# Merged RWKV and gMLP kernel: one early decay scan instead of two, weight checks in halves from the middle on, and five more constant products at the start

## The chip, the cores and the metric

The kernel runs on one core of a Trainium2 chip. The metric is the device time of one execution in microseconds (us). TensorE (PE) multiplies matrices; VectorE (DVE), ScalarE (ACT) and GpSimd (POOL) work on elements; SyncE (SP) issues nearly all DMAs. PSUM is the memory that PE writes to.

## The reference

```python
for t in range(768):                                   # batch 4, 8 heads, head size 48
    cur = einsum('bhd,bhe->bhde', u * k[t], v[t])
    y[t] = einsum('bhd,bhde->bhe', r[t], state + cur)
    state = w[t][..., None] * state + einsum('bhd,bhe->bhde', k[t], v[t])
x = y as (4, 768, 384)
h = gelu(x @ w_in)                                     # 384 -> 1024, tanh form
u_, v_ = h[..., :512], h[..., 512:]
v_n = (v_ - mean) / sqrt(var + 1e-6) * g_ln
v_s = einsum('ts,bsd->btd', w_sg, v_n) + b_sg          # mixes the 768 tokens
out = x + (u_ * v_s) @ w_out                           # 512 -> 384
```

The decays w lie between 0.8 and 0.95. w_in and w_out come in as 64-bit floats, all else as 32-bit floats.

## The kernel before

**Recurrence.** The 768 tokens of each of the 4 sequences are cut into 6 chunks of 128, which gives 24 steps, numbered 0 to 23. A step loads the decays W with a guard column ahead of each of the 4 head pairs (4 blocks of 129 columns and a closing one, 517 in all), and K and R side by side in one buffer KR. `decays` makes the products of the decays: a scan from the right writes the suffix products Suf (line 568, restarted at the guards by constants), and a second scan turns W into prefix products that start from the reciprocal of a block's whole product. `decayed_k` multiplies K by Suf (617), and the last part of `decays` multiplies R by the new W (585). PE then transposes K (`turned`, 724), multiplies K by R (`scores`, 678), forms K times V (`products`, 685) and adds up the outputs (701, 712). `own_weights` makes the term with u: for steps 0 to 3 by a product on DVE or POOL (629) and 8 small matmuls (634), later on the element engines; `masked` lays the scores over it (755).

**The second scan.** For steps 0 to 7 it runs in two halves of 258 columns. Each half has a reciprocal of 2 guards ahead of it, written into a PSUM tile called `resets`, whose other columns are zero, and the scan computes state = W * state + resets. For steps 8 to 23 it runs in one piece, with 4 reciprocals written into an SBUF tile D2 of 517 columns. Line 568 likewise takes its restart constants from `resets` (as bf16) in the early steps and from D1 in the later ones. After step 7 `resets` becomes a fourth PSUM tile for large products.

**gMLP.** Outputs of three steps make half a sequence. `taken` copies it out of PSUM, `move` shifts rows with small DMAs (918), `split_x` cuts it into a high and a low part. `v_piece`, `u_piece`, `gate_piece` and `out_piece` form every large product as three matmuls of high and low parts (950, 951, 952). For the last sequence sums of tokens replace part of the products. Weights are cut in two by `f64_weight` (DVE lines 1303 to 1311, three matmuls at 1315 to 1317 for the first six) or `f32_weight`.

**Checks.** The fast path holds for weights and decays within a range. `range_check` reads the decays of two steps again and squares and compares them on ACT (603, 605); `f64_check` reads each of the 10 pieces of the 64-bit weights again into a KR buffer and does the same (1339, 1340). Both begin after the last step's K. `verdict` adds up the counts on DVE (1263 to 1275), sums over partitions by a 1-column matmul (1278), writes `bad` (1280), and every engine loads that flag and branches (1431, 1433).

**Order.** Each function is a chain of operations, and `ORDER` lists which chain takes its next operation on which engine (S, P, D, A, G for SP, PE, DVE, ACT, POOL); every engine runs its instructions in that order. A planner in the kernel keeps an assumed time for each operation; from it come the buffer each one takes, waits of POOL on earlier DVE work, and constant matmuls with which `fill` (481) covers planned gaps of PE in the first 80 us. Ahead of all this `warm` issues `WARM[0]` constant products of 128 columns on an all-ones tile. In `own_weights` two more precede the 8 small matmuls.

Of the kernel before, what the change touches and what calls it, by code (L numbers as in the profile page):

```python
# [8 lines left out]
F32 = mybir.dt.float32  # L9
# [6 lines left out]
ALU = mybir.AluOpType  # L16
# [9 lines left out]
DM = H * D  # L26
# [17 lines left out]
f3D f3D k4S q1S k4D v1P v1A x1P D1D f3D D1D f3D e3G k4D k4D k3S k3D q2S o4S t0S t0S t0S k2P k2A H2P a3A H2A d2A j4A  # L44
v1P z2P w3P F1A F1A C0A k4D k4P k3D f3G h2S h2A h2G s2D w3D r4S x2P f4D k5S c0S D2D D2D f4D w3A f4D f4D v2P v2A p4S
C0P d3A z3P v2P e4G C0A s3D k5D k3D F2A F2A k4A k5D h0S t1S t1S t1S p5S k3D w4D k5D r5S C1A C1D w4D w5D H3P H3A h0A
j3A h0G j5A a4A K0P K0P K0P K0A H4P v3P v3A x3P w5G D3D w4D H4A w4A h1S q4S o5S h1A k3P f5D f4D D3D t2S h5S t2S t2S
K1P K1P v3P x4P f5D k5D K0D d4D f4D e5G D4D D4D f5D a5A k3A C2A C2D h1D F3A h5A F3A k5P h5D k5A h3S h3A h3G K0A K0G
K1P K1A o6S h4S h4A q5S z4P q6S p6S J1P H5P J1P H5A J1P f5D s4D v4P v4A f5D w5D w5A r6S t3S k6S o8S t3S t3S J2P J2P
J2P x5P v4P K1D K1A h4D d5D f5D D5D z5P f6D s5D f6D K0G w6G J0P J0P J0P K1G F4A F4A v5P J2A K0G K0A K1G K2P e6D J0A  # L50
k6D w6D k6D K1D k6D v5A v5P K0A C3A C3D j6A k6D K0D k6D k8S k8D o7S r7S F5A F5A t4S t4S t4S p8S k6D k8D J1A K1A K1A
K1D k8D f7D H6P H6A t5S t5S t5S C4A C4G K2P K2P j8A K2A K2D k8D e7D k8D K3P K3P K3P K3A K3D K2A K2D k8D C5A C5G J3P
J3P J3P J3A K3A a7G K3G K2G K4P x6P H7P H7A q8S D6A f6D w6D w6A K3G K2G K3G K3A K2A f6D f6D f6G K4P K4P D6D f7D f7D
f7D f7D k9S k9D f7D k9D k9D k7S q7S k9D K2A K2D w8D J4P J7P J7P J4P J4P J4A k7D k7D J7P J7A K3A K4A K4D K4A K3D j7A
k7D k7D K4D k7D p7S r9S r8S z6P s6D K4G J6P J6P J6P m1P j9A w7D K5P K5P K5P K5A K5D K5A m1P m1P m1P m0P K4D K4A k9D
k7D k9D m0P m0P m0P z7P J6A K5D w8D w7D w8D w7D K5G K5G K4A K4D f8D K5A K5A K5D m2P m3P m3P m2P m2P f8D f8D f8G w7G
m0P m3P m3P m0P m0D m0D m0A e8G m1P m1P m1D a8A m0D m1D m1A s7D p10S o9S p9S r10S f9D w8A m2P m2P m2P m2D m3P m3P J5P
d7A J5P J5P J5A m1D m2D m2A m3D m3D m3A a9A m2D f9D E6P w9G e9G w10G m3D f9D f9G u0P u1P u0P u1P u2P u1P u2P u1P u0P
u0P o10S r11S q9S F6A I8A D7D F6A s8D D7D E7P w9D w9D w9A d8A F7A I9A F7A w10D w10D f10D e10G u1D f10D f10D f10G s9D
D8D D8D w10A a10G u0D m7P m7P m7P m4P p11S o11S f11D f11D f11D f11D m7P m7P m7P m7D E8P F8A m4P F8D w11D w11D p12S u1S  # L60
r12S q10S u2P u2P w11D u2D e11G d9G m4P w12G w12G m4P m4P m4P m5P m5P m5P m5P m6P m5P m6P I10A q11S t6S t6S t6S m7D
m4D D9D m4D D9D s10D o12S w11A f12D m7A C6A a11G d10G m7D C6D f12D f12D E9P F9A I11A e12G F9A m4A C7A C7G f12G m6P m6P
m6P K6P K6P m6P m5P r13S p13S u0S o13S s11D D10D w12D q12S u2S r14S D10D m4D m6D f13D m6D f13D K6P K7P K6A m6A m6D
w12A a13G C8G C8G w13D K6G w13D f13D f13D K7P E10P J11P K7P d11G K6A K7A K7G K7A J11P J11P J8P J8P K8P K8P K8P J11A
F10D F10D D11D s12D m5D m5D K6G K6G K6G e13G f14D K7D q15S p14S o14S I12A E11P J8P r15S o15S K6A K6A K6D m5A m5D K7G
K7G K8A w13D w13D f14D F11A F11A a14A J8A I13A K8G K8A t7S t7S q13S t7S J9P u5P J9P J10P J10P J10P J10A J9P w14D f14D
K7D K7A f14D w14D s13D w14D K8G K8G K8D f15D f15D J9A K7D C9A C9D e14D C10G C10G e15G u4P K8A K8A u3P u3P u3P p16S
p15S u4P u4P u4P u4D u5P u5P u5P u3P r16S u5D u5S C11A D12A D12D K8D C11D w15D w15D K9P K9P K9P K9A K9D d13A E12P f15D
K9A K9G K9G I14A K9G w14A D13D f15D D13D q14S a15G K9A K9A u3D F12D w16D f16D s14D J15P J15P K11P K11P K11P J15P K11A
K11G F12A K11A K9D m9P K10P K10P K11D K11G w16D K10P K10A J15A r17S K10G m10P E13P K11D K11G K11G w15D w16D d14A K10A  # L70
K10G K10G F13D F13A K10D f16D m10P m10P K11G m9P m9P m10P m8P w15D K10A K10A K10D a16G o17S o16S p18S u4S p17S q16S
u3S f16D m8P m8P m8P m8P m8P m8D m8D I15A D14D D14D f17D m8A m8D s15D e16G f16G m9P m11P m11P m9P m9P m9D m9D m9A m9D
e17G f17D m11P m10P m10P m11P m11P m10D m10D m10A m10D J12P m11P m11D d15A E14P J14P J14P m11D F14D F14A u6P u6P u6P
J14P J14A w18G w16G w18G w18D f17D f17G s16D m11A m11D J12P J12P J12A u8P D15D D15D w17D I16A a17A w17D d16D r18S p20S
# [290 lines left out]
def rwkv_gmlp(ctx: ExitStack, tc: tile.TileContext, wpad, kr, vtok, ktok, vt, u, ucol, w_in, consts_, w_sgT, w_out, out):  # L365
# [196 lines left out]
    def decays(n):  # L562
# [7 lines left out]
        if early:  # L570
# [6 lines left out]
            if n == RESETS - 1:  # L577
                m_m.free.append((op.seen, resets))
# [1032 lines left out]
```

## Time and profile before

| | us |
|---|---|
| median of 3 runs (range) | 347.82 (347.13 to 348.28) |
| profiled execution: its time | 350.2 |
| profiled execution: first to last instruction (span) | 348.4 |
| PE busy | 340.0 (98%) |
| DVE / ACT / POOL busy | 273.0 / 213.5 / 148.2 |

The profiled execution took 1.8 us more than its span, and 2.4 us more than the median of the runs without a profile. A busy PE means that some matmul was under way; other engines may be idle at no cost while PE is the bound.

### The profile page before, as it was taken

How to read it: one execution, taken by the hardware profiler on the slowest of the kernel's cores; microseconds unless marked ns; L12 is line 12 of the kernel's file. 1: busy time of each engine (PE TensorE's matmuls, PEld its weight loads, DVE VectorE, ACT ScalarE, POOL GpSimd, SP SyncE). 2: the span in 40 equal slices, each digit the busy share in tenths (PEclk: the TensorE clock that was granted, in tenths of full speed). 3: DMA queues.
4: the chain of work that ended last, by engine and by line, in shares of the span. 5: the costliest groups of instructions: out<-in, count | busy, mean ns of one | idle time of the engine just before them, and what ended most of it. 6: DMA issues, size and time to landing. Idle time of an engine off the chain costs nothing.

```text
span 348.4 us, 10988 instructions
## 1 busy us (share of the span) xinstructions
PE 340.0 (98%) x4453; PEld 313.9 (90%) x4453; DVE 273.0 (78%) x541; ACT 213.5 (61%) x564; POOL 148.2 (43%) x221
## 2 busy tenths in 40 slices
PE   7999999999999999999999999999999999999994
PEld 6887688899999899889999989999999889999993
DVE  6989999998999799777889796866746365767673
ACT  1579799972664477572313375372642689897982
POOL 7356343505524541453707445144323634448400
PEclk9699999999999999999999999999999999999998
DMA  7868995614256737235256345220365454636742
GB/s 287 300 225 288 345 337 186 189 56 158 85 170 215 236 130 236 68 105 206 76 163 202 115 147 197 96 100 36 119 205 173 155 182 164 232 125 192 201 147 95
DMA packets 28470, 60.46 MB, mean 174 GB/s; under 512 B 3456, under 2 KB 13184, under 8 KB 28416
## 3 DMA queue, kind: packets, MB, share of 16 engines
q1 hardware_dynamic: 28272, 59.63, 51.5%
q8 instruction: 36, 0.59, 0.7%
q14 instruction: 18, 0.15, 0.2%
q10 hardware_dynamic: 144, 0.10, 0.1%
HBM read 53.82 MB, written 4.72 MB: 168 GB/s over the span
## 4 chain that ended last, share of the span: by engine, by line
PE 91%; ACT 3%; POOL 2%; DMA 2%; DVE 1%; issue 0%; SPq 0%; POOLq 0%; ACTq 0%
PE m_ps L950 17%; PE m_ps L952 16%; PE m_ps L951 16%; PE resets L950 6%; PE resets L951 6%; PE resets L952 6%; PE a_ps L678 5%; PE y_ps L701 4%; PE y_ps L712 3%; PE y_ps L685 2%; DMA x<-y 2%; PE m_ps L481 2%; PE m_ps L1145 1%; PE a_ps L1145 1%; PE m_ps L724 1%; PE y_ps L1145 1%
## 5 line engine op out<-in xcount | busy, mean ns | idle before, releaser
L950 PE MATMUL m_ps<-wsgh,vn 128*128 128x384 f32 x114 | 39.1, 343 | 0.0
L952 PE MATMUL m_ps<-wsgh,vn 128*128 128x384 f32 x114 | 38.4, 337 | 0.0
L951 PE MATMUL m_ps<-wsgl,vn 128*128 128x384 f32 x114 | 38.3, 336 | 0.0
L653 ACT ACTIVATE a<-KR,own 128x64 f32<-128x64 f32 x120 | 30.4, 342 | 4.1 <-DVE own L647 4.0
L617 POOL TENSOR_TENSOR KR<-KR,W 128x512 f32<-128x512 f32 x18 | 21.8, 1216 | 23.6 <-DVE W L568 8.1
L950 PE MATMUL m_ps<-g,wouth 128*128 128x384 f32 x80 | 27.3, 341 | 0.0
L952 PE MATMUL m_ps<-g,woutl 128*128 128x384 f32 x80 | 26.9, 336 | 0.0
L951 PE MATMUL m_ps<-g,wouth 128*128 128x384 f32 x80 | 26.9, 336 | 0.0
L1050 ACT CAST g<-m_ps 128x384 fp32r<-128x384 f32 x21 | 9.9, 477 | 27.0 <-DVE m_ps L1048 27.0
L950 PE MATMUL m_ps<-xT,winh 128*128 128x384 f32 x75 | 25.9, 345 | 0.0
L952 PE MATMUL m_ps<-xT,winl 128*128 128x384 f32 x75 | 25.2, 336 | 0.0
L951 PE MATMUL m_ps<-xT,winh 128*128 128x384 f32 x75 | 25.2, 336 | 0.0
L987 POOL TENSOR_TENSOR st<-st,mhalf 128x1 f32<-128x1 f32 x24 | 14.7, 613 | 20.2 <-DVE g L1322 6.3
L678 PE MATMUL a_ps<-KR 64*64 64x128 f32 (+1 forms) x768 | 22.8, 255 | 0.0
L1046 DVE SCALAR_TENSOR_TENSOR m_ps<-m_ps,flat 128x384 f32<-128x384 f32 x21 | 13.0, 618 | 12.1 <-PE m_ps L952 11.3
L950 PEld LDWEIGHTS m_ps<-wsgh,vn 128*128 128x128 f32 x114 | 21.4, 188 | 0.6
L583 DVE TENSOR_TENSOR_SCAN W<-W,D 128x516 f32<-128x516 f32 x16 | 21.4, 1337 | 0.4
L952 PEld LDWEIGHTS m_ps<-wsgh,vn 128*128 128x128 f32 x114 | 21.4, 188 | 0.3 <-DVE vn L1002 0.3
L701 PEld LDWEIGHTS y_ps<-a,vtok 64*64 64x64 f32 x768 | 16.0, 134 | 6.2 <-issue 3.9
L951 PEld LDWEIGHTS m_ps<-wsgl,vn 128*128 128x128 f32 x114 | 21.4, 188 | 0.2
L701 PE MATMUL y_ps<-a,vtok 64*64 64x64 f32 x768 | 21.2, 224 | 0.0
L585 POOL TENSOR_TENSOR KR<-KR,W 128x512 f32<-128x512 f32 x12 | 14.8, 1231 | 14.3 <-PE m_ps L952 3.7
(374 smaller groups left out, 1095.7 us busy)
## 6 DMA issues: line engine op xcount, KB each, us to landing
KR<-in_kr SPq DMA_DIRECT2D x24, 512.0 KB, 4.5
RK<-in_ktok SPq DMA_DIRECT2D x20, 384.0 KB, 4.2
W<-in_wpad SPq DMA_DIRECT2D x24, 258.5 KB, 3.1
KR<-in_wpad SPq DMA_DIRECT2D x9, 517.0 KB, 3.8
vtok<-in_vtok SPq DMA_DIRECT2D x24, 192.0 KB, 3.8
out<-o SPq DMA_DIRECT2D x21, 192.0 KB, 2.7
vn<-in_w_in SPq DMA_DIRECT2D x6, 512.0 KB, 4.8
KR<-in_w_in SPq DMA_DIRECT2D x6, 512.0 KB, 4.1
```

The costliest lines, as they stand in the source:

```text
L583: nc.vector.tensor_tensor_scan(W[:, 0:WL - 1], W[:, 0:WL - 1], D2[:, 0:WL - 1], 0.0, ALU.mult, ALU.add)
L585: engine[op.e].tensor_tensor(cols(x.R), cols(x.R), blocks(W, 0), ALU.mult)
L617: engine[op.e].tensor_tensor(cols(x.K), cols(x.K), blocks(x.Suf, 2), ALU.mult)
L653: nc.scalar.activation(a[:, j, p], eyes, AF.Copy, scale=o[:, j, p:p + 1])
L678: nc.tensor.matmul(ps_[64 * c_:64 * c_ + 64, j, p * C:p * C + (2 * T if c_ < turn else T)], x.K[rows, at:at + T], r_, start=True, stop=True)
L701: m = nc.tensor.matmul(place(y, j, q, r, c_), x.V[64 * c_:64 * c_ + 64, h * D - up(p, j):h * D - up(p, j) + 64], x.a.tile[64 * c_:64 * c_ ...
L950: nc.tensor.matmul(ps, lh, rh, start=(i == 0), stop=False)
L951: nc.tensor.matmul(ps, lh, rl, start=False, stop=False)
L952: nc.tensor.matmul(ps, ll, rh, start=False, stop=(i == n - 1))
L987: nc.gpsimd.tensor_tensor(rstd, var, c.mhalf, ALU.pow)
L1046: nc.vector.scalar_tensor_tensor(ps, ps, c.g[:, d:d + 1], c.b_bc[:, ts], ALU.mult, ALU.add)
L1145: nc.tensor.matmul(ps, x, y, start=False, stop=True, skip_group_check=True)
```

## The change

It has five parts.

1. In the early steps the second scan runs in one piece, as in the later ones. In both, the 4 reciprocals go into the guard columns of W itself, and the scan computes state = W * state + 0 from an initial 1: at the end of a block the state is its reciprocal start times the block's whole product, that is 1 up to rounding, so the next guard restarts it. The zeros come from one column of `resets` (early) or D1 (later), read with step 0. The reciprocal no longer waits for the scan of the step before, and the tile D2 with its memset leaves the recurrence.
2. `f64_check` runs on half pieces, 20 instead of 10, takes the free tile D2 instead of a KR buffer, and may start after step 8's K instead of the last step's.
3. `range_check` reads two steps in one DMA from step 2 on, not only from step 6 on (13 DMAs instead of 15).
4. `WARM` has 16 constant products instead of 11.
5. `ORDER` is another list. The engines of many operations differ in it: R times W goes to POOL 17 times instead of 12 and K times Suf 15 times instead of 18; `decayed` leaves DVE (5 times before) for POOL and ACT; the first product of step 1's `own_weights` goes from POOL to DVE; step 0's K goes from DVE to POOL and step 1's from POOL to DVE. In the first steps scores come ahead of transposes on PE, and `k0`, `o2`, `o3` are loaded earlier. At the end the verdict's 7 DVE operations ahead of its matmul come before the last pieces are finished, the 1-column matmul follows the last large one at once, and four of the last six output DMAs go to ACT's queue (one before).

```diff
-r0S o0S w0G f0D f0D f0D f0D f0D e0D r1S b0S f0G f1D k1S k1D k1D w0P w0A w0A a1A j1A o1S q0S k2S r2S H0P z0P w1G w1P
-w1A H0A w1A f1D f1D f1D k1D k1D k1P s0D f1D e1G k2D f1D k2D k0S k0D k2D k0D v0P H1P z1P s1D k0D x0P k2D k0D f2D f2D
-f2D o3S j2A j0A v0A D0A D0D H1A v0P F0A a2A F0A k1A o2S q3S k0P k0A d1A w2G w2P w2A w2A w3G e2G f2D f2D r3S f2G f3D
...
-u23P u22P u21P u22P u19S u18D u18S u23P u21P u21P u22P u23P u21P u21D u21S u22P u22D u22S u23P u23D u23S u23D u23A M0D
-M0D M0D M0D M0D M0D M0D M0P M0D
+r0S o0S r1S b0S w0G w0P w0A w0A f0D f0D f0D f0G e0G f1D f1D f1D k1S k1D o1S z0P w1D k0S q0S H0P H0A k1D s0D o2S o3S
+r2S f1G k1D e1D j1A a1A w1P w1A w1A v0P v0A z1P k1D k1P r3S k0D k0D k0D k0D j0A s1D k0P k1A f2D f2D f2D x0P k5S k0A
+a2A D0A D0D H1P H1A k2S d1A f3D q2S q1S w2G w2P w2A v0P w3G x1P e2G f2G k2D f3D k2D k5D D1D k5D k2D k5D k2D F0A F0A
+k5D e3G k4S w2A f3D v1P v1A w3P v1P H2P j5A f3G j2A F1A F1A H2A h1S h1A h1G r4S D1D k2P k2A d2A z2P o4S t0S t0S t0S
...
+J31A A1D A0A A0D u23P u21P u22P u22P A1D M0D u18D M0D A1A A1D u18S u19A M0D M0D u21P u23P u21P u23P u22P u22P u22D
+u22A u21P u21D u21A u23P u23D u23A u23D M0P u23S M0D
-WARM = (11, 80.0, 0.22)
+WARM = (16, 80.0, 0.22)
...
-    r_two = resets[:, 0:HQ]
+    r_zero = resets[:, 0:1].broadcast_to([128, WL - 1])
+    d_zero = D1[:, 1:2].broadcast_to([128, WL - 1])
-    nc.vector.memset(D2, 0.0)
...
-        if early:
-            for i in range(2):
-                at = slice(i * HQ, (i + 1) * HQ)
-                yield Op({"DVE": 0.1}, after=[ch[n - 1].e_pre] if n else [])
-                nc.vector.reciprocal(r_two[:, 0:HQ:Q], Suf[:, i * HQ + 1:(i + 1) * HQ:Q])
-                op = yield Op({"DVE": 0.64}, done=x.e_pre if i else None)
-                nc.vector.tensor_tensor_scan(W[:, at], W[:, at], r_two, 0.0, ALU.mult, ALU.add)
-            if n == RESETS - 1:
-                m_m.free.append((op.seen, resets))
-        else:
-            yield Op({"DVE": 0.12}, after=[ch[n - 1].e_pre] if n else [])
-            nc.vector.reciprocal(D2[:, 0:WL - 1:Q], Suf[:, 1:WL - 1:Q])
-            yield Op({"DVE": 1.17}, done=x.e_pre, two=True)
-            nc.vector.tensor_tensor_scan(W[:, 0:WL - 1], W[:, 0:WL - 1], D2[:, 0:WL - 1], 0.0, ALU.mult, ALU.add)
+        yield Op({"DVE": 0.12})
+        nc.vector.reciprocal(W[:, 0:WL - 1:Q], Suf[:, 1:WL - 1:Q])
+        op = yield Op({"DVE": 1.17}, after=[ch[i].e_pre for i in range(n)] if n == RESETS - 1 else [], done=x.e_pre,
+                      two=not early)
+        nc.vector.tensor_tensor_scan(W[:, 0:WL - 1], W[:, 0:WL - 1], r_zero if early else d_zero, 1.0, ALU.mult, ALU.add)
+        if n == RESETS - 1:
+            m_m.free.append((op.seen, resets))
...
-        two = n < 6
+        two = n < 2
...
-        op = yield dma(n, take=[s_kr], after=[ch[N - 1].e_k])
+        op = yield dma(n, take=[s_d2], after=[ch[RESETS].e_k])
-        yield Op({"ACT": 1.55}, free=[b], done=e_wchk[k])
+        yield Op({"ACT": 0.52 + n / 500}, free=[b], done=e_wchk[k])
...
     for k, w in enumerate(weights):
-        plan.add(f64_check(k, w[1]))
+        for i in range(2):
+            n = w[1].shape[1] // 2
+            plan.add(f64_check(2 * k + i, w[1][:, i * n:(i + 1) * n]))
```

## Rows read from the trace of the kernel before

**Rows 1.** The profile page: the chain that ended last, by engine.

```profile
PE 91%; ACT 3%; POOL 2%; DMA 2%; DVE 1%; issue 0%; SPq 0%; POOLq 0%; ACTq 0%
```

**Rows 2.** Busy time by stage: length, engines (instructions), granted clock, DMA share, GB/s.

```profile
0.00:45.00 45.00, 41.97 (x687) 34.06 (x687) 38.82 (x82) 29.29 (x97) 23.76 (x47) 0.92 0.85 292
45.00:100.00 55.00, 55.00 (x780) 49.57 (x779) 52.28 (x108) 41.88 (x119) 22.29 (x28) 1.00 0.51 168
100.00:280.00 180.00, 179.76 (x2640) 169.26 (x2639) 137.55 (x255) 88.36 (x246) 77.20 (x107) 1.00 0.45 147
280.00:343.00 63.00, 63.00 (x349) 60.98 (x347) 42.66 (x90) 54.01 (x104) 24.99 (x40) 1.00 0.54 175
```

The engines stand in the order PE, PEld (weight loads), DVE, ACT, POOL.

**Rows 3.** The same view, stretches of 2 us in the head.

```profile
6.00:8.00 2.00, 1.30 (x10) 1.11 (x10) 1.48 (x4) 0.00 (x0) 1.36 (x2) 1.00 1.00 394
8.00:10.00 2.00, 2.00 (x11) 1.79 (x10) 1.97 (x4) 1.15 (x6) 1.18 (x1) 0.52 0.80 319
...
14.00:16.00 2.00, 2.00 (x14) 1.86 (x13) 2.00 (x5) 0.23 (x2) 0.07 (x1) 0.78 1.02 390
```

**Rows 4.** The chain that ended last, head: start us, us, what.

```profile
6.11 1.26 POOL RK L629
...
11.15 3.71 PE m_ps L481 x16
...
18.76 1.31 PE m_ps L481 x10
...
31.47 6.17 DMA x<-y
```

**Rows 5.** Timeline of the head: start us, us, engine, line, what [idle before].

```profile
1.28 4.32 PE L481 MATMUL m_ps<-junk 128*128 128x128 f32 x22 [1.28 <-POOL junk L458]
...
3.84 1.23 DVE L568 TENSOR_TENSOR_SCAN W<-W,resets 128x516 f32<-128x516 f32 x1 [0.86 <-DMA W<-in_wpad]
...
5.10 0.17 DVE L574 RECIPROCAL resets<-W 128x2 f32<-128x2 f32 x1
...
6.24 0.69 DVE L576 TENSOR_TENSOR_SCAN W<-W,resets 128x258 f32<-128x258 f32 x1
...
9.14 0.49 DVE L1303 TENSOR_SCALAR vn<-vn 128x512 int32<-128x512 int32 x1
...
9.66 0.69 DVE L1305 SCALAR_TENSOR_TENSOR vn<-vn,vn 128x512 int32<-128x512 int32 x1
...
18.06 0.69 PE L678 MATMUL a_ps<-KR 64*64 64x64 f32 x32
...
18.89 0.74 DVE L755 COPY_PREDICATED a<-mask,a_ps 128x512 f32<-128x512 uint8 x1 [2.07 <-ACT winh L1328]
...
40.42 1.22 DVE L568 TENSOR_TENSOR_SCAN W<-W,resets 128x516 f32<-128x516 f32 x1
```

**Rows 6.** Single lines, the full-width scans: count, ns min/median/max, first and last start.

```profile
L568 DVE TENSOR_TENSOR_SCAN W<-W,resets x8: 1202/1222/1229, 3.8 to 60.6; 128x516 f32<-128x516 f32 x8
...
L583 DVE TENSOR_TENSOR_SCAN W<-W,D x16: 1220/1226/2058, 83.1 to 237.7; 128x516 f32<-128x516 f32 x16
```

**Rows 7.** ACT by line and shape, weight checks: busy us, mean ns, idle before.

```profile
L1340 ACT ACTIVATE KR<-KR,hmin 128x512 f32<-128x512 f32 x6 | 4.6, 769 | 0.2
L1339 ACT ACTIVATE KR<-KR 128x512 f32<-128x512 f32 x6 | 4.0, 670 | 3.2 <-DMA KR<-in_w_in 3.2
...
L1339 ACT ACTIVATE KR<-KR 128x384 f32<-128x384 f32 x4 | 2.2, 561 | 5.0 <-DMA KR<-in_w_out 5.0
```

**Rows 8.** The chain that ended last, its end.

```profile
343.73 0.09 DVE chk L1263
...
344.91 0.15 DVE bad L1280
```

**Rows 9.** The line of the branch, SP's part: count, ns, first and last start.

```profile
L1433 SPq EVENT_SEMAPHORE  x8: 17/17/17, 346.1 to 346.7; - x8
```

**Rows 10.** DMA issues from 342 us on: count, KB each, us to landing.

```profile
out<-u ACTq DMA_DIRECT2D x1, 96.0 KB, 1.9
```

More of the change, by code (lines that the diff above doesn't have):

```diff
@@ L46 @@
[L46 to L50, printed above, removed]
@@ new lines @@
+D3D f5D D3D f5D j3A a4A v3P a5A d4A x4P K0D k3D K0A w4D K1P K1P h4S h4A p5S k3D k3P e5G w5G D4D w4D w4A F3A F3A f5D
+f5G k4D D4D h3S h2S t2S t2S t2S k3D h5S o8S r6S q5S h4D C2A C2D w5D p6S q6S h3A h3D K1P K0G K0G K0G H5P z4P w5D s4D
+K1A H5A K1D h5A h5D k5P k5A h2A h2G d5A J2P J2P J0P J0P v4P x5P f6D D5D v4D f6D f6D K2P K2P z5P v4P w6G w6D o6S k6S
+t3S t3S r7S t3S w5A K0A s5D F4A F4A K0A J2P J2A K2P w6D f6G k8S v5P v5A e6D k6D K0D k6D K1A K1D C3G f7D J0P J0A J1P
+t4S t4S t4S K1G v5P k6D K2A C3D F5A F5A j6A k6D o7S r8S t5S J3P H6P H6A K2D K2A k8D k6D f7D K1G C4A K1A K1A k6D f7D
@@ new lines @@
+J1P J1P J3P K2G K2G K2G K2A C4D t5S t5S k8D k8D K1D k8D j8A C5A C5D k8D J3P x6P K3P K3P K3P K3A K3D k8D K2A J3A K2D
+K3A K3D f8D K3G D6A D6D f8D q8S k7S k7D k7D p7S q7S p8S K4P K4P K4P K4A J6P J6P J6P J6A J4P J4P w6A k7D K4D k7D K4A
+K3D e7D w8D K4D K4G J5P J4P J4A j7A z6P K5P K5P K3A K3A J1A a7A J5P J5P J5A H7P K5P s6D f7D k7D K4D K3D w7D k9S z7P
+m1P m1P m1P k9D k7D k9D r9S K5A a8A K5D j9A k9D k9D k9D k9D w7D K5A H7A K5D w8D w7D K5G K5G m0P m1P m0P m0P m0P K4A
+K4A f9D K4D f9D f8D K5A K5A K5D w7A m3P m3P w8D w8A s7D m2P m3P m2P m2P m2P f8G p10S o9S p9S m2P m0P m3P m3P m0P m0D
@@ new lines @@
+u10P u10P u10D e20G K12P u9P J18P u9P u9P K12P u9D J16P J16P e21D I19D K14D f21D p22S i19S t9S q20S D18A t9S t9S u10S
+r22S J16P J16A D18D K12P K12A K12D d19G C15G K12A a21A J17P J17P J17P J17A u11P u11P u11P u11P C15D K12G K12G C16A
+u11D C16G E18P w22D K13D C17A C17D K15P K15P f21D F18D F18D J18A i19A K12G K12G K12A K15P K15A I20D w21A s20D f22D
+f22D D19D D19D i8S r23S q21S o22S w23G w23D w23D K15D K15A K17P K17P J20P J20P J20P J20A K17P K16P K16P K16P K12D E19P
+J22P J22P J22P K15D K15G K15G K16A a22A K16D d20G K15A f22D K15A K15D f22D K16A K17A D20D D20D e22G d21A J22A K17G
@@ new lines @@
+K17A J23P J23P K16D K16G m17P m17P J23P J23A m18P s21D f23D F19D F19D I21A m16P m17P m16P E20P m19P m16P K17G K16G
+f23D K17G K17D K16G K16A w22D w22D K16D K17A K17A K17G F20A i8A w22D f23D s22D m18P m18P m18P m16P m16P m19P m18P m18P
+F20D m18D m18D m16P m16D m19P m19P m16D u11S o23S q22S i18S i18A I22A m18A m16A m17P m17P m17P m19P m19P D21D D21D
+m17D m17D d22A m17A e23G f23G m19D m19D m16D y6S w23G t10S t10S i13S i13A y6A m19A y6A E21P u14P m17D u9S y8S q23S
+t10S i2S i2A y8A a23G g0S g0S m18D y8A m19D J21P u12P u12P u12P u12P u12D u12S y11S i3S i3A u13P u13P u14P u14P u14P
@@ L1265, in verdict @@
         nc.vector.tensor_reduce(cnt[:, 0:1], chk, AX.X, ALU.add)
-        nw = 2 * KT + FT
+        nw = 2 * (2 * KT + FT)
         yield Op({"DVE": 0.1}, after=e_wchk)
         nc.vector.tensor_scalar(wchk[:, 0], wchk[:, 0], HMAX * HMAX, None, ALU.is_lt)
-        for k0, k1, n in ((0, 2 * KT, FF), (2 * KT, nw, DM)):
+        for k0, k1, n in ((0, 4 * KT, FF // 2), (4 * KT, nw, DM // 2)):
             yield Op({"DVE": 0.1})
@@ L1285, in rwkv_gmlp @@
     e_wout = [Event() for _ in range(FT)]
-    e_wchk = [Event() for _ in range(2 * KT + FT)]
+    e_wchk = [Event() for _ in range(2 * (2 * KT + FT))]
     e_u, e_uc = Event(), Event()
```

104 lines of the change are left out of this document (44 added, 60 removed).

## Prediction

> **What bounds the kernel now.** I read the chain of waits first, for the engine that sets the end. PE holds 91% of it [rows 1]. The busy time by stage says where: from 45 us to 343 us PE idles for 0.24 us in all, although DVE has 52.28 of 55 us of work up to 100 us and ACT 54.01 of 63 us at the end [rows 2]. The change takes no large matmul away, so in this long middle part a faster DVE or ACT gives nothing. What can be won lies in the head, in the tail, and in what PE does there that is no work.
>
> The 2-us stretches of the head come next. PE runs out of constant products at 5.60 us (1.28 + 4.32) [rows 5] and is busy for only 1.30 of the 2 us from 6 to 8; right after 8 us the granted clock falls from 1.00 to the lower level (1.2 GHz instead of 2.4), and comes back at about 14.9 us (0.78 as the mean of 14 to 16) [rows 3]. During these 6.8 us PE is busy all the time, but at half speed, so some 3.4 us of its work are lost. The chain shows what this delays: the 16 constant products of 11.15 to 14.86, at 0.23 us each instead of 0.13 (1.31 us for 10 at full clock), which stand in PE's queue ahead of step 1's small matmuls [rows 4]. Step 1's scores come only at 18.06, and DVE, which has the most work in the head, idles for 2.07 us until it can mask them at 18.89 [rows 5]. The profile puts this wait down to ACT; the scores in DVE's input are PE's.
>
> Later in the head the chain passes over ACT and over one row-shifting DMA of 6.17 us at 31.47 [rows 4], with the DMA engines busy for 0.85 of the first 45 us [rows 2].
>
> **The change part by part.**
>
> *Five more constant products.* 11 products show as 22 instructions [rows 5], so 5 are 10, and 10 take 1.31 us at full clock [rows 4]. They end near 6.9 us. The two products of `own_weights` that follow (4 instructions, 0.52 us) bring PE to 7.43, while the product that the small matmuls need is ready at 7.37 (6.11 + 1.26) [rows 4]. So they fill the gap and cost at most 0.1 us there; if PE were needed at 5.6 they would cost 1.3. Whether the clock then holds is not shown by a run; the bounds are nothing and the whole loss, 3.4 us of PE work. I take it that it holds, since the gap ahead of the fall is what they close. What the kernel gets back is bounded by the engine that waited, DVE: 2.07 us.
>
> On this the Trainium skill (TensorE: Matmul & The Clock Gate, Part 1: The HAM clock gate) says that low speed is the default and activity lifts it, and that the gate judges activity in a rhythm of its own, not tied to the kernel's start, so that the same kernel can change level at another point in another run. The fall after the idle stretch in this trace agrees with the first; of the second one trace shows nothing. By it the five products need not help in every run, which is the first rival below.
>
> *The second scan in one piece.* An early step spends 2 x 0.17 on reciprocals and 2 x 0.69 on half scans, 1.72 us. Afterwards it spends 0.17 on one reciprocal and one scan of 516 columns. That operand pair, W from SBUF and one PSUM column read over and over, has no row. The nearest are the first scan with `resets` (1.222) and the late second scan (1.226) [rows 6]; they differ by nothing although one reads bf16 from PSUM and the other 32-bit numbers from SBUF, so I take 1.22. The bounds are 1.20 (the lowest of these) and 1.38 (two halves). That saves 0.33 us a step, 0.2 to 0.35 with the bounds, 2.6 us over 8 steps. Six of the 8 begin in the head, from 3.84 to 40.42 [rows 5]: 2.0 us of DVE. The late steps keep their 1.226. The memset of D2 that goes was hidden, as DVE waited 0.86 us for W anyway [rows 5].
>
> *Order in the head.* With these durations I laid the new list out by hand. Step 0's decays end at 6.5; step 1's follow at once (DVE waited for no second W before) and end at 9.2. Then come eight operations on the first two weight pieces, 0.4 to 0.7 us each (line 1303 0.49, line 1305 0.69) and 4.5 in all, and three more of about 0.7: the product for step 1 that POOL made before, step 0's mask (0.74) and step 1's K [rows 5]. So step 1's scores are masked at about 15.9, where before it was 18.89. Part of this is work put off: before, DVE had by then done two operations fewer on the second weight piece and three on another one. Continued in this way, with equal work done, DVE is some 2 us ahead at 28 us.
>
> *What the head gives.* DVE idle time removed, 2.07, plus 2.0 of scans: at most 4.1 us. Not all reaches PE, since later in the head ACT and the DMAs set the pace. I take 2.6, between the 2 us that the layout by hand shows and this bound, nearer to the first.
>
> *Tail.* The chain ends with the verdict on DVE from 343.73 to 345.06 [rows 8]. With only the last operation (0.15) left after the last output piece, the flag is there at about 343.9, 1.15 us earlier. But SP must also wait for the last output. It is issued at about 343.75 and takes 1.9 us [rows 10]: 345.65, where SP's final waits began at 346.1 [rows 9]. So DMA is late next, and the gain is 0.45; bounds 0.2 and 1.15.
>
> *Weight checks in halves.* The two passes over a piece of 512 take 0.67 and 0.77 us, and the first of them 0.56 at 384 columns [rows 7], so 128 columns are 0.11 us and a pass over 256 some 0.45, which is 0.11 more than half. 20 halves with two passes make ACT 4.5 us busier, and there are 20 more short reads of the sums. In the new list 17 of the 20 come in its first three quarters, during the steps. There ACT is busy for 88.36 of the 180 us from 100 to 280 [rows 2], which covers them; without that cover each would cost over 1 us. I take 0 and keep up to 4 for waits (third rival). The last 60 us lose ACT work, where PE waited for nothing anyway: 0.
>
> *The rest.* Two DMAs fewer for range checks, ten more issues for the half checks, R products moved to POOL and `decayed` moved off DVE: hidden behind PE as long as PE's queue is fed, 0, with +0.5 as a bound.
>
> **The sum.** 2.6 + 0.45 = 3.05 us off the profiled execution's 350.2 (span 348.4 and 1.8 around it), so 347.15 there. The median of the runs shown is 2.4 lower; the same difference takes 347.82 to 344.8. Within 0.3% means 1.04 us: from 346.78 to 348.86.
>
> **The rivals.**
>
> - *The clock falls again*, in the head's second half or because PE idles while step 0's K is on POOL (two products of about 1.2 us in a row). Then DVE's idle time comes back and about half of the scans' 2.0 remains, with the tail 1.45 off or less: 346.4 to 347.4. For it speaks that PE's work in the head is small and scattered; against it, that planned gaps are filled. 0.14.
> - *The head is set by DMA.* The 6.17 us transfer stays where it is, and what DVE gains ends in a wait for it: only the tail is left, 347.4. For it: DMA share 0.85. Against: the step outputs that it moves are ready earlier. 0.08.
> - *Checks block ACT in the middle, slower.* ACT runs its list in order; before, the 10 checks stood ahead of their data for 8.2 us together [rows 7], at places where PE had work queued. With one D2 for 20 checks, SP's queue waits for ACT's last check too, and loads behind it come late. If the 20 wait as long each, 0.82 us, that is 16 us, and half of it reaching PE is 8: 344.8 + 8 = 353, and 350 already at a third. It decides from the point where PE waits for over 4.1 us in the middle (3.05 + 1.04). Against it: ACT's idle share there and 0.24 us of PE idle time. 0.11.
> - *Everything counts*: 4.1 in the head and 1.15 at the end, 342.6. Against it: the output's 1.9 us. 0.10.
>
> **The numbers.** The forecast has 0.57, with a range of its own from 343.5 to 346.3. The range from 342.9 to 347.9 takes in the first two rivals and most of the last, and leaves out the slower one and the far end of the last. Faster: 0.57 + 0.10 + half of the first rival, 0.74. Same: the other half and the second, 0.15. Slower: 0.11.
>
> **What would show it.** Granted clock 1.00 from 8 to 15 us; one scan of about 1.22 us per early step; step 1's masking near 16; PE without gaps from about 42 us; one verdict operation after the last output; half checks with no PE wait after 100 us. I am wrong if the clock falls again, if PE waits on ACT or a DMA in the middle, or if full PE time moves by less than 1 us.

## The result: 1.2% slower

| | before | after |
|---|---|---|
| median, us (executions) | 347.98 (8) | 352.59 (8) |
| range, us | 347.13 to 350.25 | 350.01 to 354.50 |
| profiled execution: time / span | 350.2 / 348.4 | 354.5 / 352.8 |

The ratio is 1.0115 (95% interval 1.0074 to 1.0156); it is taken of the means, 4.0 us apart, while the medians are 4.6 us apart. The forecast was 344.8, faster; what came lies near the third rival's price of 353, in part by luck, as the account below shows. The profiled execution of after is the longest of its 8, so its losses are somewhat larger than the typical ones.

**Where the time went.** The busy time by stage, in the columns of [rows 2], for after:

```profile
0.00:45.00 45.00, 41.71 (x732) 34.17 (x733) 41.39 (x75) 32.15 (x102) 25.85 (x50) 1.00 0.92 312
45.00:100.00 55.00, 54.79 (x764) 49.76 (x762) 50.16 (x103) 42.06 (x122) 20.81 (x26) 1.00 0.50 168
100.00:280.00 180.00, 175.53 (x2588) 164.65 (x2589) 129.56 (x245) 99.58 (x291) 76.01 (x101) 0.99 0.49 156
280.00:343.00 63.00, 63.00 (x349) 61.07 (x348) 43.79 (x94) 47.81 (x100) 27.38 (x45) 1.00 0.40 129
```

PE now idles for 4.47 us from 100 to 280 us, where it idled for 0.24 [rows 2], and for 0.21 before that. In the head the clock now holds (1.00 instead of 0.92), with about the same busy time. The 2-us stretches of the head, beside [rows 3], and of the worst place:

```profile
6.00:8.00 2.00, 2.00 (x21) 2.00 (x20) 1.93 (x4) 0.00 (x0) 1.92 (x3) 1.00 0.96 348
8.00:10.00 2.00, 1.92 (x21) 1.73 (x24) 1.97 (x2) 1.28 (x6) 1.83 (x2) 1.00 0.97 333
14.00:16.00 2.00, 2.00 (x38) 1.36 (x30) 1.90 (x5) 1.33 (x5) 0.00 (x0) 1.00 0.97 343
264.00:266.00 2.00, 1.48 (x9) 1.16 (x7) 0.87 (x2) 0.00 (x0) 0.00 (x0) 1.00 0.48 105
266.00:268.00 2.00, 0.00 (x0) 0.00 (x0) 0.28 (x2) 1.80 (x6) 0.00 (x0) 1.00 0.69 243
268.00:270.00 2.00, 1.81 (x57) 1.68 (x61) 1.11 (x3) 2.00 (x4) 0.40 (x1) 0.70 0.16 34
270.00:272.00 2.00, 2.00 (x37) 1.88 (x32) 0.97 (x3) 1.42 (x4) 1.57 (x2) 0.50 0.46 170
272.00:274.00 2.00, 2.00 (x12) 1.96 (x12) 0.51 (x2) 1.97 (x3) 1.81 (x2) 0.94 0.31 94
```

From 266 to 268 us PE does nothing at all, and after that the granted clock falls to its lower level: the missing shares of 268 to 274, (0.30 + 0.50 + 0.06) x 2 us, are 1.7 us more. With 4.23 + 0.21 us of added idle time that makes 6.1 us in this execution.

**What stands there.** The chain of waits through that place (start us, us, what):

```profile
255.92 4.42 DMA D<-in_w_in
...
260.36 0.54 ACT D L1332 x2
...
261.56 4.58 DMA D<-in_w_in
...
266.16 0.53 ACT D L1332 x2
...
267.33 0.37 ACT x L372
...
267.72 0.30 DVE y L372
...
268.07 0.51 PE y_ps L694 x16
```

and the timeline of the same place, with the idle time before an operation in brackets:

```profile
260.36 0.44 ACT L1332 ACTIVATE D<-D 128x256 f32<-128x256 f32 x1 [4.70 <-DMA D<-in_w_in]
...
261.45 1.14 ACT L596 ACTIVATE KR<-KR,wmid 128x1024 f32<-128x1024 f32 x1
...
266.16 0.43 ACT L1332 ACTIVATE D<-D 128x256 f32<-128x256 f32 x1 [2.30 <-DMA D<-in_w_in]
...
268.07 0.46 PE L694 MATMUL y_ps<-a,vtok 64*64 64x64 f32 x16 [2.59 <-DVE y L372]
```

Two half checks, one soon after the other. ACT has the first pass of a check next in its list and waits 4.70 us for the data; as soon as its passes have freed the one tile D2, SP issues the next half. ACT runs a range check's passes meanwhile (from 261.45) and then waits another 2.30 us for that half. Behind its passes in ACT's list stands the copy of a step's output out of PSUM (267.33), then DVE's copy, then PE's next accumulation, for which PE waits 2.59 us. Of the remaining 1.63 us of idle time in the middle 1.5 lie in two gaps from 99.8 to 105.7 us (1.10 us, begun shortly before 100, and 0.63), for which the profile names no cause. The cost over the whole kernel is in the groups of instructions (busy us, mean ns, idle time before):

```profile
L1332 ACT ACTIVATE D<-D 128x256 f32<-128x256 f32 (+1 forms) x20 | 8.3, 414 | 25.9 <-DMA D<-in_w_in 19.1
```

25.9 us of ACT's time in 9 waits, on average 1.3 us for each half check; the whole pieces took 8.2 us for ten [rows 7]. Halving a piece shortens the wait for it little or not at all: the DMA issues (KB each, us from issue to landing) show 4.1 us for half a piece of w_in and 2.9 for half a piece of w_out in after, and below, in before, 4.1 and 3.9 us for whole ones.

```profile
D<-in_w_in SPq DMA_DIRECT2D x12, 256.0 KB, 4.1
...
D<-in_w_out SPq DMA_DIRECT2D x8, 192.0 KB, 2.9
```

```profile
KR<-in_w_in SPq DMA_DIRECT2D x6, 512.0 KB, 4.1
...
KR<-in_w_out SPq DMA_DIRECT2D x4, 384.0 KB, 3.9
```

### The profile page after: what moved, and what is told of

The parts are those of the page before. It is cut to its first block, busy times and chain, and to the rows that moved or that the text cites. A ratio compares the mean times of both kernels' runs of the same rounds, so it can differ in the third digit from the quotient of the medians.

```text
span 352.8 us, 11066 instructions
## 1 busy us (share of the span) xinstructions
PE 340.3 (96%) x4459; PEld 314.5 (89%) x4459; DVE 268.9 (76%) x526; ACT 222.1 (63%) x614; POOL 150.0 (43%) x222
## 4 chain that ended last, share of the span: by engine, by line
PE 88%; DMA 3%; DVE 3%; issue 1%; POOL 1%; ACT 1%; SPq 1%; DVEq 0%
PE m_ps L943 16%; PE m_ps L944 15%; PE m_ps L945 15%; PE resets L943 6%; PE a_ps L671 5%; PE resets L944 5%; PE resets L945 5%; PE y_ps L694 4%; PE y_ps L705 3%; DMA D<-in_w_in 3%; PE y_ps L678 2%; PE m_ps L1308 1%; DVE W L568 1%; PE m_ps L1138 1%; PE m_ps L717 1%
## 5 line engine op out<-in xcount | busy, mean ns | idle before, releaser
L943 PE MATMUL m_ps<-wsgh,vn 128*128 128x384 f32 x111 | 37.8, 341 | 0.0
L945 PE MATMUL m_ps<-wsgh,vn 128*128 128x384 f32 x111 | 37.3, 336 | 0.0
L646 ACT ACTIVATE a<-KR,own 128x64 f32<-128x64 f32 x128 | 32.2, 338 | 1.6 <-DVE W L571 1.4
L1332 ACT ACTIVATE D<-D 128x256 f32<-128x256 f32 (+1 forms) x20 | 8.3, 414 | 25.9 <-DMA D<-in_w_in 19.1
L944 PE MATMUL m_ps<-g,wouth 128*128 128x384 f32 x68 | 22.9, 337 | 0.1
L943 PE MATMUL m_ps<-g,wouth 128*128 128x384 f32 x68 | 23.0, 338 | 0.0
L943 PE MATMUL m_ps<-xT,winh 128*128 128x384 f32 x66 | 22.9, 346 | 0.0
L945 PE MATMUL m_ps<-g,woutl 128*128 128x384 f32 x68 | 22.8, 335 | 0.0
L945 PE MATMUL m_ps<-xT,winl 128*128 128x384 f32 x66 | 22.2, 336 | 0.0
L944 PE MATMUL m_ps<-xT,winh 128*128 128x384 f32 x66 | 22.1, 335 | 0.0
L943 PE MATMUL m_ps<-winh,xT 128*128 128x512 f32 x54 | 22.1, 409 | 0.0
L671 PEld LDWEIGHTS a_ps<-KR 64*64 64x64 f32 x768 | 18.5, 134 | 3.4 <-issue 1.9
L944 PE MATMUL m_ps<-winl,xT 128*128 128x512 f32 x54 | 21.3, 394 | 0.0
```

What stands on the lines that cost most here:

```text
L646: nc.scalar.activation(a[:, j, p], eyes, AF.Copy, scale=o[:, j, p:p + 1])
L671: nc.tensor.matmul(ps_[64 * c_:64 * c_ + 64, j, p * C:p * C + (2 * T if c_ < turn else T)], x.K[rows, at:at + T], r_, start=True, stop=True)
L943: nc.tensor.matmul(ps, lh, rh, start=(i == 0), stop=False)
L944: nc.tensor.matmul(ps, lh, rl, start=False, stop=False)
L945: nc.tensor.matmul(ps, ll, rh, start=False, stop=(i == n - 1))
L1332: nc.scalar.activation(sq, sq, AF.Square, accum_out=wchk[:, 0, k:k + 1])
```

## The experiments

Medians of the executions stand beside those of the kernel before, taken between them on the same chip; an interval is of the ratio to it. A single profiled execution is called so.

### Products and scans, each alone

The kernel before with 16 constant products, and the kernel before with the new scans (part 1):

```diff
-WARM = (11, 80.0, 0.22)
+WARM = (16, 80.0, 0.22)
```

> The kernel before with 16 constant products first in place of 11, nothing else. Theory (they close the gap ahead of the fall, and the clock holds): granted clock 1.00 from 8 to 15 us, DVE's wait of 2.07 us at 18.9 is gone or under 1 us, 1 to 2 us off, 346 to 347 where before takes 347.9. Rival (the clock falls later in the head all the same, or the head is set by DMA): within 0.5 us of before.

> The kernel before with the new scans alone: one reciprocal and one scan in the early steps, restarts in the guards of W in all steps; the words of the second half scans are taken out of the order. Theory (DVE sets the head): 0.33 us less DVE work in an early step, half of 2.0 us reaches the end, 346.6 to 347.4. Rival (PE at half clock sets the head up to 23 us, then ACT and a DMA): within 0.4 us of before.

Measured: 348.87 (1.001, 0.9983 to 1.0037) and 348.44 (1.001, 0.9987 to 1.0032), before 348.11. Neither gains. The scan itself is as forecast, in the view of that line of after (ns min/median/max, first and last start): 

```profile
L574 DVE TENSOR_TENSOR_SCAN W<-W,resets x8: 1217/1228/1229, 5.1 to 58.2; 128x516 f32<-128x516 f32 x8
```

But PE doesn't see it. The chain of the kernel with the scans alone has the row-shifting DMA where before had it [rows 4], and it takes longer:

```profile
29.29 6.76 DMA x<-y
```

It ends at 36.05; PE idles for 1.26 us from 35 to 45 us. In the three profiles of before that is 0.65, 0.38 and 1.32 us (the second and third are those of the next section), with the same DMA in the chain each time (6.17, 5.90 and 7.04 us).

### The kernel before, again

Two more single executions of the unchanged kernel:

> The kernel before, unchanged, profiled once more. Theory (the profiled execution shown of before was one in which the clock fell in the head, and most executions are not such): granted clock 1.00 from 8 to 15 us, span near 346 us and the last output piece on DVE done near 341.5, some 2 us ahead of the profile shown. Rival (the fall at 8 us belongs to this kernel): clock near 0.5 from 8 to 15 us and a span of 348 us again.

> The kernel before, unchanged, for one more profile to set beside the new order's. If the typical execution holds the clock in the head, it ends its last output piece near 341 to 342 us with the clock at 1.00 from 8 to 16 us; if the profile shown was the typical one, near 343.7 with the clock at the lower level there.

Measured: 348.64 and 348.54. The stretch from 8 to 16 us, first and second:

```profile
8.00:16.00 8.00, 7.78 (x83) 6.63 (x86) 7.86 (x16) 4.31 (x18) 3.66 (x3) 0.79 0.93 322
```

```profile
8.00:16.00 8.00, 7.78 (x124) 6.38 (x124) 7.86 (x16) 5.77 (x22) 3.67 (x3) 1.00 0.92 318
```

The same kernel shows clocks of 0.79 and 1.00 there; over the same stretch it was 0.57 in the execution behind [rows 3]. DVE's wait of 2.07 us ahead of step 1's mask [rows 5] is 0.78 us in the first, and in the second there is none:

```profile
17.60 0.73 DVE L755 COPY_PREDICATED a<-mask,a_ps 128x512 f32<-128x512 uint8 x1 [0.78 <-ACT winh L1328]
```

The span is 346.8 in both, 1.6 less than in that one, and their times are again 1.7 to 1.8 above the span. So the profiled execution shown before the prediction was a rare one. The mean clock over the whole span, known of every execution, was 0.987 in it; of the 107 executions of before under 360 us that stand beside the experiments, 6 were at 0.988 or lower, with a median of 350.1, and the 67 above 0.9965 had 347.83. If a mean clock as low as that stands for the full fall, it costs 2.3 us when it comes, and it comes in one of 18; where in those 6 executions the clock fell isn't known.

### After without the checks' parts

Three kernels take the half checks apart. One without the 20 DMAs and the 40 ACT passes, one with the DMAs alone, one with the passes alone (over a constant that D2 was filled with at the start); in all three the weights are not checked.

```diff
-        nc.scalar.activation(sq, sq, AF.Square, accum_out=wchk[:, 0, k:k + 1])
-        nc.scalar.activation(sq, sq, AF.Sign, bias=hmin, accum_out=wchk[:, 1, k:k + 1])
```

is the main part of the DMAs alone, and of the passes alone

```diff
-        nc.sync.dma_start(raw, src)
```

> The changed kernel without the 20 half weight checks: neither their DMAs nor their ACT work are done, and their counts are set to constants that pass. Theory (half checks stand in ACT's list ahead of their data and hold up the copies that PE waits for): PE idle time from 100 to 280 us falls from 4.47 to under 1 us, the clock does not fall there, and the time comes to 345 to 346.5. Rival (the middle loses its time to the new order of the other work, such as R products on POOL): PE still idles for 3 us or more there, and the time stays at 351 to 353.

> The changed kernel with the 20 DMAs of the half checks at their places, but without their ACT work; the counts are constants that pass. It has as many SP instructions as the changed kernel. Theory (ACT's list held by checks is what costs in the middle): PE idle time from 100 to 280 us under 1 us, no fall of the clock there, DVE's last output piece done near 342.3 as in the run without checks, and a time of 347.5 to 348.8. Rival (the DMAs behind each other on SP's queue delay loads): PE still idles for 2 us or more in the middle, 350 to 352.

> The changed kernel with the 40 ACT passes of the half checks at their places, but without the 20 DMAs: they run over numbers already in D2, so there is no data to wait for (the weights are left unchecked). If the wait for data is the cause, ACT's idle time ahead of the passes goes, PE idles for under 1 us from 100 to 280 us, and the time is 349 to 350. If ACT's 18 us of added passes themselves delay the copies that PE waits for, it stays at 351.5 to 352.6.

Measured: without both 351.39 (1.0095, 1.0065 to 1.0125), DMAs alone 349.50 (1.0031, 1.0000 to 1.0062), passes alone 349.56 (1.0039, 1.0011 to 1.0066). The last two each take 3.0 us off the median of 352.6 (2.9 and 2.6 of the 4.0 us by the ratios to before), and PE idles for 0.37 us from 100 to 280 us in both. The row of the kernel with the passes alone, to be set beside that of after:

```profile
100.00:280.00 180.00, 179.63 (x2610) 168.63 (x2603) 131.03 (x249) 102.43 (x294) 79.78 (x107) 1.00 0.42 136
```

ACT is busier than in after (102.43 against 99.58) and PE hardly waits: neither ACT's added work nor the added transfers cost PE anything in the middle. What costs is ACT standing ahead of data that is not there. SP's queue, the other one that waits, hardly explains it: with the DMAs alone SP still stands 15.5 us at the checks' DMAs, until an earlier one has landed in D2 (total us, times, longest).

```profile
SPq L1330 <- DMA D<-in_w_out: 8.5, 3, 5.1
SPq L1330 <- DMA D<-in_w_in: 7.0, 2, 5.4
```

The kernel without both has a clean middle too (PE idles for 0.37 us from 100 to 280) and its last output piece is done at 342.34, yet it isn't faster. The reason stands after its work, on SP (line of the branch: count, ns, first and last start):

```profile
L1427 SPq EVENT_SEMAPHORE  x8: 17/17/17, 347.3 to 347.8; - x8
L1427 SPq COMPARE_BRANCH  x1: 70/70/70, 344.2 to 344.2; - x1
```

3.1 us from the branch to the final waits, where after has 0.6 (350.3 to 350.9). So its time says nothing on the checks. What fills this gap stays open.

### Spread out

After with the 20 checks spread evenly, 38 places of the list between each DMA and its passes (two of the 20 are shown), and then the same for the first 17 with 36 places:

```diff
-... r11S i16S i16A F7A ... q9S i6S i6A o11S ...
+... w9G i16S w9G E7P ... u0P i16A u1P ... E8P i6S D9D ... f12D i6A C6G ...
```

> The changed kernel with all 20 half checks, spread evenly over the middle of the order, each ACT pass some 7 us behind its own DMA issue and ahead of the next one. Theory (the wait for the data is what costs): ACT's wait for check data falls from 25.9 us to under 5, PE idle time in the middle to under 1 us, 345.5 to 347. Rival (the additional ACT work of about 9 us, or the smaller DMAs, cost the time): 350 to 353, as the work and the DMAs are all there.

> The changed kernel with only the 17 early half checks spread, each ACT pass some 36 places of the order behind its DMA issue; the last three stay where the changed kernel has them. Theory: no wait of ACT for check data before 300 us, PE idle under 1 us from 100 to 280 and under 0.5 from 280 to 340, 347 to 349. Rival (9 us more ACT work cost the time wherever they stand): 351 to 353.

Measured: 353.63 (1.0145, 1.0093 to 1.0197) and 356.20 (1.0242, 1.0221 to 1.0262). My expectation fell: ACT waits 1.5 us in all for the data of these checks in the second and not at all in the first, instead of 25.9, and still the second takes longer than after; the first lies within its interval. The waits of SP's queue in the second (total us, times, longest) show where the wait went:

```profile
SPq L1329 <- ACT D L1333: 38.9, 12, 8.0
```

and in after:

```profile
SPq L1329 <- ACT D L1333: 13.6, 9, 3.3
```

With the passes put late, the one D2 comes free late, and SP stands at the next check's DMA for up to 8 us with all loads, outputs and the fences between PE's groups (line 660, a no-operation on SP that PE waits for) behind it in its list. PE's waits in that kernel begin with

```profile
PE y_ps L678 <- SPq L660: 3.3, 3, 1.5
```

and its chain has an output DMA of 4.91 us at 134.39, issued late, for whose buffer DVE waits. In the first of the two a range check's load came late in the same way (6.33 us at 304.37), ACT waited for it, and PE idled for 1.81 us from 300 to 320 with a clock of 0.91.

### Part 2 put on and taken off

After with part 2 alone undone: 10 whole checks in KR buffers, from the last step's K on, at places that I chose among the range checks. And the order of before with the new scans and the half checks at the places where after has them.

```diff
-        op = yield dma(n, take=[s_d2], after=[ch[RESETS].e_k])
+        op = yield dma(n, take=[s_kr], after=[ch[N - 1].e_k])
...
-        for i in range(2):
-            n = w[1].shape[1] // 2
-            plan.add(f64_check(2 * k + i, w[1][:, i * n:(i + 1) * n]))
+        plan.add(f64_check(k, w[1]))
```

> The changed kernel with part 2 alone undone: 10 whole weight checks in KR buffers, none before the last step's K, each issued 9 to 30 places of the list ahead of its ACT passes. If the half checks in the middle are the cause of the loss, PE idles for under 1 us from 100 to 280 us, the clock stays at 1.00 there, and the time is that of before less the 0.64 us of the tail: 347.4 (346.8 to 348.2). If the new order costs by itself, in the head or in the middle, it stays near the 349.5 of the kernel that had the check DMAs without the ACT passes.

> The order of before with the new scans (348.4 without more) and the 20 half checks put where the changed order has them. If waits for their data on ACT and for the one tile D2 on SP are the cause, PE idles for 3 to 6 us between 100 and 320 us and the time is 351 to 353. If the checks hurt only through the other places of the new order, it stays within 348 to 349.

Measured: 357.63 (1.0280, 1.0243 to 1.0318) and 358.72 (1.0315, 1.0266 to 1.0364), before 347.79. The second goes the way of the theory, and further: the order of before with the scans, 348.44 without, loses 10 us to half checks at places that weren't laid out for it. PE idles for 6.5 us from 100 to 280 us, most of it at one place in its chain, again a check ahead of what PE needs (`v` is an activation of a large product):

```profile
207.36 3.15 DMA D<-in_w_in
210.54 0.53 ACT D L1332 x2
211.09 0.61 ACT D L1333 x2
211.70 0.58 ACT v L972 x2
212.33 0.56 PE resets L943
```

The first fell, and teaches the same. Its middle is clean up to 260 us (0.13 us of PE idle time from 100), but whole checks at my places do later what the halves did earlier:

```profile
260.39 0.33 SPq L1328
...
260.77 3.68 DMA out<-o
...
264.54 0.57 DVE o L1248
...
265.13 0.02 ACT x L371
```

SP issued a check only when ACT had freed a buffer, the output behind it landed 3.68 us later, DVE waited for that buffer, and ACT's copy and PE's products for DVE. So it is not the half as such, nor the middle as such, but where a check stands in the lists of SP and ACT. That whole checks at good places would leave after without loss isn't shown.

### The tail

After with the verdict at the very end as before (single execution), and the kernel before with the new scans and the early verdict:

```diff
-... B0D M0D B0A ... u20S M0D u19D B0D M0D ... A1D M0D u18D M0D ... u19A M0D M0D u21P ... u23D M0P u23S M0D
+... B0D B0A ... u20S u19D B0D ... A1D u18D ... u19A u21P ... u23D u23S M0D M0D M0D M0D M0D M0D M0D M0P M0D
```

and, for the other,

```diff
-... y7S J30P ... J30A B1D ... A0A i6S u20S i6A B1D ... A1D y7A y7A u23P ... u21D ... u22D ... u23P u23D u23S u23D u23A M0D M0D M0D M0D M0D M0D M0D M0P M0D
+... y7S i6S J30P ... J30A i6A y7A y7A B1D ... A0A u20S B1D ... A1D u23P ... M0D M0D M0D M0D u21D ... M0D M0D M0D u22D ... u23P M0P u23D u23S u23D u23A M0D
```

> The changed kernel with the verdict at the end as before: its 7 DVE operations, matmul and flag after the last output piece. What is read is the stretch from the end of DVE's last output piece to the end of the span: 4.0 us in the changed kernel, 4.65 in the kernel before. Theory (the output's landing is late next, so most of the 1.15 us of verdict are lost again): 4.6 to 4.7 us. Rival (the rest of the gain comes from the outputs on ACT's queue): 4.0 to 4.3 us.

> The order of before with the new scans (348.4 without more), and the tail of the change alone: the 7 verdict operations ahead of the 1-column matmul come before the last output pieces are finished, the matmul right after the last large one. If the tail's gain is its own, last output piece to end of the span takes 4.0 us instead of 4.65 and the time is 347.8, 0.64 less than without it. If the earlier last checks on ACT delay the last copies, or the verdict's operations the last pieces on DVE, it stays at 348.4 or above.

Measured: 351.26, and 354.23 (1.0193, 1.0150 to 1.0236). From the end of the last output piece to the end of the span it is 4.65 us in the first (344.85 to 349.50), 4.65 in before (343.73 [rows 8] to 348.4), 4.0 in after (348.78 to 352.8), and 3.8 in the second (348.14 to 351.9). So the early verdict gives 0.65 to 0.85; the first has four of the last six outputs on ACT's queue as after has, and they alone gain nothing. But, in the second, to have the counts in time I had moved the last two checks of before's list ahead, and ACT ran them in front of the casts that the last products need:

```profile
336.82 1.14 ACT L595 ACTIVATE KR<-KR,wmid 128x1024 f32<-128x1024 f32 x1
337.99 1.15 ACT L597 ACTIVATE KR<-KR,whalf 128x1024 f32<-128x1024 f32 x1
339.04 0.19 ACT L597 ACTIVATION_READ_ACCUMULATOR KR<-KR,whalf 128x1 f32 x1
339.13 0.46 ACT L1042 CAST g<-y_ps 128x384 fp32r<-128x384 f32 x1
```

PE idled for 2.72 us from 320 to 343, and the clock fell after that (0.83 from 340 to 350 us): the gain was paid for several times over.

### What stays when the waits are gone

349.5 is still 1.5 above before (1.4 and 1.8 above the medians beside them), although the tail is shorter. The kernel with the ACT passes alone was profiled twice more, and run with 11 products:

> The same kernel as the one with the ACT passes alone (no check DMAs), once more profiled, since its profile was of its fastest execution. If the rest of the loss (349.56 against 347.79) lies in the new order's head, an execution near 349.5 shows more PE idle time from 16 to 45 us than the 2.71 us of the first profile; if it lies in the middle, more than 0.4 us from 45 to 280; if it is the clock, a stretch below 1.00.

> As the one ahead of it, a third profile of the same kernel: PE idle time from 16 to 45 us above 2.71 us if the rest lies in the head; above 0.4 us from 45 to 280 us if it lies in the middle.

> The changed kernel with the ACT passes but no check DMAs (349.56), and 11 constant products instead of 16. If the five products are what holds the clock in the new order's head, the granted clock falls after 8 us and the time is 350.5 to 352; if they only delay PE's first real work, it is 0.5 to 1 us less, 348.8; if they do nothing, 349.5.

Measured on another chip, with before at 348.17: 348.53 and 347.76 (single executions), and 348.50 with 11 products (1.0011, 0.9997 to 1.0025). PE idled for 2.05 and 0.86 us from 16 to 45 (1.71 in the first profile; the 2.71 of the expectation is a slip), for 0.37 from 45 to 280 in both, and the clock held from 8 to 16. An execution as long as 349.5 was not caught in a profile. The one with 11 products again shows the lower clock at 8 to 16 us (0.79), so in the new order, too, the products hold it. Whether the 1.5 us are the chip's, the head's or the five products' is not settled.

### Toward a faster kernel

Two kernels have the order of before, the new scans and the early verdict, with one weight check moved out of ACT's last 8 us: as two halves through D2, each issued 60 places ahead of its passes. The second has 16 products as well.

```diff
-... A0A i6S u20S i6A ... A1A A1D y7A y7A ... u18D ... u23P u23D u23S u23D u23A M0D M0D M0D M0D M0D M0D M0D M0P M0D
+... i9S ... i9A ... i10S ... i10A ... A0A y7A u20S ... A1A y7A A1D ... M0D M0D M0D M0D M0D M0D M0D M0D u18D ... u23P M0P u23D u23S u23D u23A M0D
```

> The order of before with the new scans (348.4 without more), the verdict's operations on DVE before the last output pieces, and room made for that on ACT: the sixth weight check, which stood in the last 8 us, goes as two halves through the free tile D2 in the middle, each issued 60 places of the list ahead of its passes and far from the other. If only waits for data and for D2 make half checks costly, these two cost nothing (PE idle from 100 to 280 us under 0.5 us), the last output piece to the end takes 4.0 us instead of 4.65, and the time is 0.64 less: 347.5. If any half check in the middle costs, or the verdict's 1.0 us on DVE delays the last pieces, it is 348.2 or more.

> The kernel with the order of before, the new scans and the early verdict (348.8, with executions from 347.2 to 349.9 by the clock), with 16 constant products instead of 11. If the spread of that kernel is the clock falling in some executions and the products prevent it, no execution has the full fall (a mean clock of 0.987), the middle of the runs moves to that of the undisturbed ones, 347.3, and it beats before by 0.2%. If the products delay the head by as much as they save, it stays at 348 to 349.

Measured: 348.80 (1.0010, 0.9984 to 1.0036) with before at 348.17, and 348.77 (1.0011, 0.9992 to 1.0029) with before at 348.58. In the first PE idles for 0.24 us from 100 to 280: two half checks that nothing waits for cost nothing. Last piece to end is 3.84 us. Its three executions with a mean clock of 1.000 took 347.22 to 347.33; the three fastest of before beside them took 347.33 to 347.54, so no gain of 0.6 shows even there. And 7 of the 12 were below 0.995 and took 348.7 to 351.7. With 16 products none of 11 was below 0.997, and none was below 348.33: the spread went, and the low end with it. Its profile has a gap of 1.2 us on PE at 103 us, again without a named cause and ahead of its first half check (185 us). Neither beats the kernel before. Where the second loses 1 us against the best executions of the first isn't shown, as none of those was profiled.

## Why the prediction was wrong

**The step that failed** is "I take 0 and keep up to 4 for waits" for the weight checks in halves. I had let ACT's idle share cover them (88.36 busy of 180 us [rows 2]). An idle share says that there is time, not that it lies where the list has the passes: ACT waited 25.9 us for the 20 halves, and the two of them at 256 to 267 us cost 2.84 of the 4.47 us (PE's idle time from 260 to 280). Removing the data wait gave 3.0 of the 4.6 us back, in two ways. The added work on ACT, 4.5 us in the sum, was 8.9 (5.1 in the passes, and 3.8 in the short reads, which had no price), and cost nothing that PE shows. The third rival had the mechanism: its 0.82 us of waiting for a check were 1.3, and its chance of 0.11 was far too small. That its 353 came out near the time is luck: it set 8 us for the checks against a head and tail 3.05 us faster, where the checks' waits cost 3.0 us in the median and the head gave nothing. Of SP's list it had said that loads behind a waiting check come late, and the spread-out checks showed just that.

**The head's 2.6 us** came to nothing: DVE's last output piece is done at 342.7 and 342.2 us in the two kernels whose middle is clean (DMAs alone, passes alone), and at 342.2 in both later profiles of before. The clock: the five products do hold it, in all 12 profiles of kernels with 16 of them, while it fell, for all or part of the stretch from 8 to 16 us, in 5 of 8 with 11; but the 2.07 us of DVE idle time belonged to a fall of full length; it was 0.78 us and nothing in the two later executions of before, and only one of 18 had a mean clock as low. The Trainium skill (TensorE: Matmul & The Clock Gate, Part 1: The HAM clock gate) says that the gate's rhythm is not tied to the kernel's start, so that the same kernel can change level elsewhere in another run; the three profiles of before, with 0.57, 0.79 and 1.00, agree. I cited this and still carried the whole gain over to the median. Its companion was "the same difference takes 347.82 to 344.8": the 2.4 us between the profiled execution and the median were for the most part not what a profile adds (the later profiled executions are 0.57 and 0.37 above the medians beside them), but that clock fall, and I counted it twice, once as the difference and once as the gain. The scans: 0.33 us a step was right, but in the order of before the chain passes over the DMA of 6 to 7 us at 29 us with the new scans as without them, the second rival, to which I had given a chance of 0.08. In after's own profile the chain does not pass over it; there PE idles for 1.82 us from 16 to 45 us, where the three profiles of before have 0.65, 0.38 and 1.89, and its longest wait, which ends at 21.93, is put down to DVE:

```profile
PE a_ps L678 <- DVE W L571: 1.1, 1, 1.1
```

So the new order has a wait of its own in the head; which of its moves made it, and whether it is what keeps the scans' gain from PE, was not tested.

**Right** were: one scan of 1.23 us per early step; step 1's masking near 16 (16.45); one verdict operation after the last output; and the size of the tail, 0.65 where 0.45 stood (0.2 to 1.15). What is late next there is not the output's landing, though. The last output is issued at 348.80 and lands some 1.9 us later, at 350.7; SP loads the flag only behind that issue, at 349.2, for 0.77 us (0.48 in before), branches at 350.3 and begins its final waits at 350.9, each of 17 ns. The late scans cost nothing in the kernel with the new scans alone; the fewer range checks and the changed engines were not run alone.

**The sum as it came out**, for the profiled execution of after against the two later spans of before: 346.8 + 4.23 + 0.21 of PE idle time + 1.7 of clock - 0.65 of tail is 352.3; the span is 352.8, which leaves 0.5 for the head. For the medians: 3.0 of 4.6 us are the checks' waits, and the other 1.6, with the tail's gain in it, stays open.

## What to carry to other kernels

- Work added to an idle engine is free only if its data is there when its turn comes; a list that runs in order turns a late load into idle time for everything behind it. Read the time from issue to landing off the trace and put the pass at least that far behind the DMA.
- With one buffer for many such pieces that wait was not placed away here: pass early and the compute engine waits for the data, pass late and the DMA queue waits for the buffer, with all its other loads behind it. Two pieces far from each other, each 60 places behind its DMA, cost nothing.
- Before a wait seen in one profile is booked as a gain, ask whether the median has it too: the mean clock of the other executions said here that it hadn't.

## What the runs showed of the hardware

- 256 KB took 4.1 us from issue to landing and 512 KB the same, 192 KB 2.9 and 384 KB 3.9, at these loads of the queues.
- After one idle stretch of 2.6 us on PE in a stage of small matmuls the granted clock was 0.70, 0.50 and 0.94 in the three 2-us stretches from 268 us on, a further 1.7 us: a stall can cost more than its length. At the same place in after with the late verdict PE waited 1.8 us, and the clock stayed at 1.00.
- In the kernel without weight checks SP took 3.1 us from its branch to its next instructions, 0.6 in after, though only DMAs and ACT passes had been taken out far ahead of it.
